# Linear-attention sums for pairs of heads in 32-column blocks, with a second ring of output tiles and a new instruction order

## The chip, the cores and the metric

The kernel runs on one NeuronCore of one Trainium2 chip. The metric is device time in microseconds (us) of one execution, as the median over the executions of one job. A median is over all executions of its job. With one core there are no dies to compare; the mean granted clock of TensorE was 0.981 in the profiled run of the kernel before.

Engines in the profile: PE is TensorE (matrix products), PEld its weight loads, DVE is VectorE, ACT ScalarE, POOL GpSimd, SP SyncE, which here only issues transfers. A name with q is the engine's sequencer or queue.

## The reference, cut to what matters

Four attention layers on x of 2048 x 512, with 32 heads of 16 columns, each behind a layer norm and with a residual. Layers A are softmax attention over a window of 256 positions; layers B are linear attention:

```python
def _B_ref(x, wqkv, wo):
    ...                                        # H = 32 heads, Dh = 16
    phi = lambda t: jnp.where(t > 0, t + 1, jnp.exp(t)) + 1e-6
    pq, pk = phi(q), phi(k)
    kv = jnp.einsum("bhsd,bhse->bhde", pk, v)  # per head a 16 x 16 sum over all positions
    z = jnp.einsum("bhsd->bhd", pk)            # per head the sum of pk
    num = jnp.einsum("bhqd,bhde->bhqe", pq, kv)
    den = jnp.einsum("bhqd,bhd->bhq", pq, z)[..., None] + 1e-6
    ...
x = A_x
x = x + _A_ref(_layernorm(x), A_wqkv, A_wo)
x = x + _B_ref(_layernorm(x), B_wqkv, B_wo)
x = x + _A_ref(_layernorm(x), A_wqkv, A_wo)
x = x + _B_ref(_layernorm(x), B_wqkv, B_wo)
```

The change concerns `kv` and `z` of the two B layers. Only the 16 x 16 blocks of one head are needed, out of the whole 512 x 512 product of pk and v.

## The kernel before

The program is a list of about 2,600 small operations. A planner issues them in the order that a constant text, `ORDER`, lays down (an operation's number, then its engine: P, A, V, G, S). It also keeps a rough clock of its own. Where that clock sees TensorE idle for over 0.45 us, it adds *fillers*: matmuls of the identity whose result nobody reads and which are to keep TensorE's clock up. And it gives each operation one of eight PSUM banks, the one free the earliest by that clock.

```python
        order = ORDER.split()
        for x in order:
            ...
            for s in o.takes:
                start = s.ring.free_at(s, start)[0]      # a PSUM bank or a buffer
            start = max(start, free[e])
            ...
            if e == "PE":
                if start - free["PE"] > self.GAP:        # GAP = .45 us
                    ...
                    fill = (b[0], m) if m else fill
            ...
            self.fill(*fill)
            o.fn(e)
```

The key-value sums of two 128-row tiles form one unit. It computes, for each of four 128-column tiles c, the full 128 x 128 product of pk and v and one column of ones behind it (129 columns), in two halves, each in a PSUM bank of its own and each with its own addition into the float32 sums in SBUF:

```python
        def kv_unit(i):
            ins = [kv_in[i + n] for n in range(2)]
            for jj in range(2):
                s = bank()
                ...
                    for tt in range(2):
                        c = 2 * jj + tt
                        for n in range(2):
                            nc.tensor.matmul(t["t"][:, tt, :], lhsT=ins[n][0][0]["t"][:, c * P:(c + 1) * P],
                                             rhs=ins[n][1][0]["t"][:, c, :], start=(n == 0), stop=(n == 1))
                ...
                    nc.vector.tensor_tensor(kvs[jj][:], t["t"][:], kvs[jj][:], op=ALU.add)
```

Later a block mask (`bd`) keeps the heads' own blocks. The last layer writes its 16 output tiles from one ring of four staging tiles:

```python
            if final:
                ost = slot("xn")
                ...
                pl.op({"SP": .4}, lambda e: nc.sync.dma_start(o_dram[i], t["o"][:]), deps=[r], use=[ost])
```

## Time and profile before

| | before |
|---|---|
| time, median of 3 runs | 477.78 us (477.42 to 478.20) |
| span of the profiled run, granted clock | 477.3 us, 0.981 |
| TensorE busy | 445.7 us, 93% |
| fillers | 48 |
| key-value matmuls, their additions | 128 of 129 columns, 32 of 258 columns |
| TensorE's last matmul ends | 468.8 us |

The prediction below shows the busy shares, the windows and the end. What it names without showing are the large groups and the waits around a shared PSUM bank. In the first fence each line is line of source, engine, operation, output<-input, count, then busy us and mean ns of one, then idle time before them and what ended it.

```profile
L834 ACT ACTIVATE pt<-psb 128x1536 bf16<-128x1536 f32 (+2 forms) x246 | 285.5, 1216 | 32.9 <-PE psb L816 25.1
L816 PE MATMUL psb<-qT,kbd 32*128 32x320 bf16 (+4 forms) x1440 | 94.3, 255 | 4.4 <-ACT pt L834 3.9
L895 PE MATMUL psb<-vbd,pt 128*128 128x34 bf16 x2880 | 84.4, 179 | 0.7 <-POOL pt L867 0.7
```

The 246 exponentials of layers A (L834) take 285.5 us of ScalarE. They come at a steady pace along both A layers, so the start of the 20th, 40th and so on is a good milestone for how far a run has come; I use it below. The B layers' work is laid between them and behind them. The second fence, of the view of waits, has: engine, line, waited for what, us in all, times, longest.

```profile
DVE ost L738 <- DMA out_dram<-ost: 5.8, 5, 2.0
ACT kbd L771 <- DVE kbd L773: 5.1, 2, 3.1
```

The first is the end's wait for a free staging tile. The second is ScalarE waiting for VectorE's half of one bank.

### The profile page before, as it was taken

To read this page: it belongs to the slowest core of one execution; us is meant where nothing else is said; L and a number is where in the kernel's file an instruction comes from. 1 tells how busy PE (TensorE), PEld (TensorE's weight loads), DVE (VectorE), ACT (ScalarE), POOL (GpSimd) and SP (SyncE) were. 2 spreads that over 40 slices of the span, in tenths; PEclk is the share of its full clock that TensorE was granted. 3 is DMA by queue.
4 is the path that set the end of the run, shared out by engine and by line. 5 is a ranking of instruction groups with operands and counts; after the bars stand their busy time and mean duration, and the time that the engine had idled before them with its cause. 6 is when DMAs were issued, how large, how long until landed. Compare 5 with 4: busy or idle time off the path is not lost.

```text
span 477.3 us, 14496 instructions
## 1 busy us (share of the span) xinstructions
PE 445.7 (93%) x5668; PEld 231.3 (48%) x5730; DVE 376.8 (79%) x987; ACT 379.1 (79%) x446; POOL 250.3 (52%) x746
## 2 busy tenths in 40 slices
PE   7789999899999999999999998999999999999991
PEld 2334554464555465543445553545546464655330
DVE  6768787778878977896988786788888887788872
ACT  7488888899998999666578996989988899876610
POOL 4256644547674765351137665477684685561141
PEclk9889999899999999999999998999999999999998
DMA  6313245103240210100010123112411311000023
GB/s 220 111 38 82 58 110 128 35 3 74 50 50 17 43 34 3 46 0 1 6 43 14 26 52 73 29 34 46 71 36 25 57 37 23 2 1 1 0 79 106
DMA packets 53805, 22.27 MB, mean 47 GB/s; under 512 B 38368, under 2 KB 53216, under 8 KB 53728
## 3 DMA queue, kind: packets, MB, share of 16 engines
q1 hardware_dynamic: 49760, 16.80, 16.9%
q10 hardware_dynamic: 3968, 4.46, 3.0%
q8 instruction: 47, 0.77, 0.7%
q14 instruction: 30, 0.25, 0.2%
HBM read 6.29 MB, written 2.10 MB: 18 GB/s over the span
## 4 chain that ended last, share of the span: by engine, by line
PE 71%; DVE 8%; ACT 7%; DMA 6%; POOL 3%; issue 3%; ACTq 0%; SPq 0%; another core or an unknown queue 0%; DVEq 0%; POOLq 0%
PE psb L563 38%; PE psb L895 13%; PE psb L816 13%; ACT pt L834 4%; DMA xnT<-xn 3%; DMA out_dram<-ost 2%; PE psb L1020 2%; POOL pt L867 1%; PE psb L1088 1%; DMA oT<-o_sb 1%; DVE vbd L542 1%; DVE pqT L1119 1%; PE psb L582 1%; PE psb L489 1%; DVE xres L745 1%
## 5 line engine op out<-in xcount | busy, mean ns | idle before, releaser
L834 ACT ACTIVATE pt<-psb 128x1536 bf16<-128x1536 f32 (+2 forms) x246 | 285.5, 1216 | 32.9 <-PE psb L816 25.1
L867 POOL TENSOR_SCALAR_AFFINE_SELECT pt<-pt 128x192 bf16<-128x192 bf16 (+2 forms) x514 | 152.7, 329 | 120.8 <-ACT pt L834 118.6
L816 PE MATMUL psb<-qT,kbd 32*128 32x320 bf16 (+4 forms) x1440 | 94.3, 255 | 4.4 <-ACT pt L834 3.9
L895 PEld LDWEIGHTS <-pt 128*128 128x128 bf16 x2880 | 78.4, 96 | 14.4 <-issue 8.9
L895 PE MATMUL psb<-vbd,pt 128*128 128x34 bf16 x2880 | 84.4, 179 | 0.7 <-POOL pt L867 0.7
L862 DVE TENSOR_TENSOR pt<-pt,tri 128x128 bf16<-128x128 bf16 (+4 forms) x268 | 65.6, 274 | 15.3 <-ACT pt L834 14.0
L816 PEld LDWEIGHTS <-kbd 32*128 32x128 bf16 x1440 | 39.7, 93 | 67.6 <-issue 59.2
L563 PE MATMUL psb<-xnT,wA 128*128 128x512 bf16 x239 | 65.5, 394 | 6.1 <-ACT kbd L771 2.4
L563 PE MATMUL psb<-wB,xnT 128*128 128x512 bf16 x240 | 62.5, 380 | 1.3 <-DVE xnT L585 0.3
L563 PEld LDWEIGHTS <-xnT 128*128 128x128 bf16 x384 | 33.4, 98 | 39.8 <-issue 9.0
L971 ACT ACTIVATE phi_e<-psb 128x512 bf16<-128x512 f32 x64 | 38.1, 603 | 17.1 <-PE psb L563 14.0
L773 DVE TENSOR_TENSOR kbd<-psb,eo 128x512 bf16<-128x512 f32 x57 | 37.1, 681 | 2.7 <-ACT kbd L771 1.9
L563 PEld LDWEIGHTS <-wA 128*128 128x128 bf16 x256 | 21.8, 99 | 34.1 <-issue 15.3
L563 PE MATMUL psb<-wA,xnT 128*128 128x512 bf16 x118 | 33.7, 399 | 1.0 <-DVE xnT L585 0.4
L563 PE MATMUL psb<-woA,oT 128*128 128x512 bf16 x118 | 32.1, 381 | 2.7 <-DMA oT<-o_sb 1.1
L563 PE MATMUL psb<-wkv,pqT 128*128 128x512 bf16 x124 | 30.0, 380 | 2.2 <-DVE ost L738 1.7
L563 PE MATMUL psb<-xnT,wB 128*128 128x512 bf16 x123 | 31.0, 380 | 0.2
L684 DVE BATCH_NORM_STATS2 ln_st<-xres 128x6 f32<-128x512 f32 (+1 forms) x39 | 26.5, 679 | 2.0 <-DMA xres<-in_A_x_dram 1.9
L974 DVE TENSOR_SCALAR phi_e<-phi_e 128x512 bf16<-128x512 bf16 x57 | 18.6, 329 | 9.6 <-ACT phi_e L971 9.2
L910 DVE TENSOR_TENSOR o_sb<-psb,rall 128x384 bf16<-128x384 f32 (+1 forms) x48 | 24.6, 513 | 1.6
L550 DVE CAST qT<-psb 128x512 bf16<-128x512 f32 x27 | 18.5, 686 | 8.0 <-PE psb L563 7.8
L977 DVE SCALAR_TENSOR_TENSOR pqT<-psb,phi_e 128x512 bf16<-128x512 f32 x32 | 21.8, 688 | 1.5 <-POOL phi_e L974 1.0
(121 smaller groups left out, 492.0 us busy)
## 6 DMA issues: line engine op xcount, KB each, us to landing
vbd<-vst SPq DMA_DIRECT2D x128, 34.0 KB, 1.9
out_dram<-ost SPq DMA_DIRECT2D x16, 128.0 KB, 1.8
wB<-in_B_wqkv_dram ACTq DMA_DIRECT2D x1, 1536.0 KB, 7.7
xres<-in_A_x_dram ACTq DMA_DIRECT2D x1, 1024.0 KB, 5.0
xnT<-xn SPq DMA_TRANSPOSE x40, 2.5
wA<-in_A_wqkv_dram SPq DMA_DIRECT2D x1, 512.0 KB, 6.7
xres<-in_A_x_dram SPq DMA_DIRECT2D x1, 512.0 KB, 7.7
woA<-in_A_wo_dram ACTq DMA_DIRECT2D x1, 512.0 KB, 3.5
```

The source lines that it names most:

```text
L563: nc.tensor.matmul(t["t"][:], lhsT=lhs(c), rhs=rhs(c), start=(c == 0), stop=(c == NCT - 1))
L684: nc.vector.bn_stats(t["st"][:], x())
L773: nc.vector.tensor_tensor(kbd[r][:, t, :, :, :].rearrange("p m k h -> p (m k) h"), ps()[:, hf * 256:(hf + 1) * 256].unsqueeze(2).to_broadc ...
L816: nc.tensor.matmul(A[:, x, at[x]:at[x] + w, :], lhsT=kbd[half(m)][32 * rg:32 * rg + 32, tt, m % 4, :, :], rhs=qT[I % 2][32 * rg:32 * rg + ...
L834: nc.scalar.activation(body[:, x:y, 0:pos[x], :], t["A"][:, x:y, 0:pos[x], :], ACT.Exp, scale=0.25)
L862: nc.vector.tensor_tensor(v, v, mt, op=ALU.mult)
L867: nc.gpsimd.affine_select(out=v, in_=v, compare_op=ALU.is_ge, fill=0.0, base=1 if kind == 0 else -2, pattern=[[0, n], [2 * sg, 64]], chann ...
L895: nc.tensor.matmul(t["O"][:, u, g, :, :], lhsT=PT[:, s0:s0 + 2, :], rhs=vbd[half(m)][:, m % 4, :, grp[g], :], start=(n == 0), stop=(n == l ...
L910: nc.vector.tensor_tensor(o_sb[:, u0:u0 + nu, h0 * DH:(h0 + 2 * ng) * DH].rearrange("p u (h e) -> p u h e", e=DH), Ov[:, :, :, 0:DH], r.to ...
L971: nc.scalar.activation(t["e"][:], ps()[:], ACT.Exp)
L974: (nc.vector if e == "DVE" else nc.gpsimd).tensor_scalar(t["e"][:], t["e"][:], 1.0, 1e-6, op0=ALU.min, op1=ALU.add)
L977: nc.vector.scalar_tensor_tensor(out=dst(), in0=ps()[:], scalar=1.0 + 1e-6, in1=t["e"][:], op0=ALU.add, op1=ALU.max)
```

## The change

The intent has three parts. First, the sums are computed only for pairs of heads: for each group of 32 columns a 32 x 32 product and one column of ones (33 columns), in the four column groups of TensorE's array (`tile_position`), so that a unit's result of 132 columns fits in one bank and needs one addition. The column of ones is written once. Second, outputs alternate between two rings of four staging tiles. Third, the whole order is new, and the planner's clock now has it that two engines are not in one bank at once, that an output tile is free only when its transfer has landed (`LAND`), and a few corrected durations.

```diff
-    WIN, FULL, GAP = 3.413, 2750, .45
+    WIN, FULL, GAP, LAND = 3.413, 2750, .45, 1.8
...
+            for s in o.slots:
+                if s.ring is self.banks and s.last and s.last.eng != e:
+                    start = max(start, s.last.end + self.LAT[s.last.eng])
...
 ORDER = """
-19H 17H 18H 20H 36V 37G 46V 6G 47G 12A 51A 41V 42G 23H 38V ...      (all 2,614 operations)
+20H 17H 36V 19H 18H 41V 46V 37G 38V 23H 12A 10V 42G 47G 51A ...      (all 2,582 operations)
...
-        kvs = [fp.tile([P, 2, P + 1], F32, name=f"kvs{j}") for j in range(2)]
+        kvs = fp.tile([P, NCT, 33], F32, name="kvs")
+        vss = [fp.tile([P, NP, 33], BF, name=f"vs{k}") for k in range(3)]
+        for k in range(3):
+            nc.vector.memset(vss[k][:, :, 32:33], 1.0)
...
-                ost = slot("xn")
+                ost = slot(("xn", "oT")[i % 2])
...
-                nc.gpsimd.memset(t["t"][:, :, P:P + 1], 1.0)
...
-            for jj in range(2):
-                s = bank()                                   # [the unit shown above]
+            s = bank()
+                for c in range(NCT):
+                    for g in range(4):
                         for n in range(2):
+                            nc.tensor.matmul(t["t"][32 * g:32 * g + 32, c, :], lhsT=ins[n][0][0]["t"][:, c * P + 32 * g:c * P + 32 * g + 32],
+                                             rhs=ins[n][1][0]["t"][:, 4 * c + g, :], start=(n == 0), stop=(n == 1), tile_position=(0, 32 * g))
...
+                    nc.vector.tensor_tensor(kvs[:], t["t"][:], kvs[:], op=ALU.add)
```

## The prediction

> **What bounds the kernel now.** I read the granted clock first (0.981, one core, so nothing to compare between dies), then the page's busy shares and slices, then the table of windows, the waits, the chain of waits, and last the timeline of the end.
>
> ```profile
> PE 445.7 (93%) x5668; PEld 231.3 (48%) x5730; DVE 376.8 (79%) x987; ACT 379.1 (79%) x446; POOL 250.3 (52%) x746
> ...
> PE   7789999899999999999999998999999999999991
> DVE  6768787778878977896988786788888887788872
> ACT  7488888899998999666578996989988899876610
> ```
>
> TensorE is over 90% busy in nearly every slice except the first three and the last; no other engine is. A busy PE row is modelled, so I checked it against start times in the trace: two 512-column matmuls follow each other every 216 ns, two of the 34-column value products (L895) every 25 ns. Taking such a pace for each form, I counted as a stall whatever exceeds it by more than 0.3 us: 33 stalls, 24.0 us, of which 8.1 us lie before 36 us. So in the middle there is little waiting to win; it is at both ends, and in what TensorE is given to do.
>
> ```profile
> 0.00:60.00 60.00, 50.95 (x540) 23.96 (x547) 44.63 (x112) 45.69 (x61) 29.82 (x110) 0.94 0.37 101
> ...
> 120.00:180.00 60.00, 58.53 (x928) 32.96 (x936) 49.51 (x140) 55.76 (x58) 39.49 (x119) 1.00 0.23 38
> 180.00:240.00 60.00, 58.78 (x494) 28.94 (x501) 49.66 (x124) 40.81 (x75) 20.94 (x51) 1.00 0.04 12
> ...
> 420.00:478.00 58.00, 46.44 (x239) 20.33 (x241) 40.65 (x79) 24.87 (x49) 16.18 (x26) 0.96 0.12 38
> ```
>
> Columns: length, busy us of PE, PEld, DVE, ACT, POOL, clock, DMA. Even where the layers meet (180 to 240) PE is 58.8 of 60, but part of this is filler work (L489, identity matmuls that keep the clock up). The end has 11.6 us without PE.
>
> ```profile
> PE 71%; DVE 8%; ACT 7%; DMA 6%; POOL 3%; issue 3%; ACTq 0%; SPq 0%; another core or an unknown queue 0%; DVEq 0%; POOLq 0%
> ...
> L489 PE MATMUL psb<-identb 128*128 128x512 bf16 x48 | 15.2, 430 | 1.5 <-POOL identb L417 1.5
> ...
> L1020 PE MATMUL psb<-vs,pks 128*128 128x129 bf16 x128 | 11.4, 221 | 0.1
> L1027 DVE TENSOR_TENSOR kvs<-psb,kvs 128x258 f32<-128x258 f32 x28 | 11.5, 421 | 5.4 <-PE psb L1020 5.3
> L1000 POOL MEMSET vs<- x32: 109/114/118, 132.2 to 435.7; 128x4 bf16 x32
> ...
> 466.17 1.29 DVE L738 TENSOR_TENSOR ost<-psb,xres 128x512 bf16<-128x512 f32 x2 [2.00 <-DMA out_dram<-ost]
> 466.92 1.89 PE L563 MATMUL psb<-wkv,pqT 128*128 128x512 bf16 x8 [1.67 <-DVE ost L738]
> 468.72 0.69 DVE L738 TENSOR_TENSOR ost<-psb,xres 128x512 bf16<-128x512 f32 x1 [1.26 <-DMA out_dram<-ost]
> ...
> 469.77 0.69 DVE L738 TENSOR_TENSOR ost<-psb,xres 128x512 bf16<-128x512 f32 x1 [0.36 <-DMA out_dram<-ost]
> 472.05 0.69 DVE L738 TENSOR_TENSOR ost<-psb,xres 128x512 bf16<-128x512 f32 x1 [1.59 <-DMA out_dram<-ost]
> ```
>
> The first line is the page's chain of waits, the next three are groups by line (busy us, mean ns, idle before), the fifth is of the view of the tile vs, the rest is the timeline of the end. The chain is TensorE to 71%. The kvs groups are what the change replaces. The last lines show the end: output tiles wait for an earlier output's transfer to free one of four staging tiles, and at 466.92 even TensorE waits behind that.
>
> **What the Trainium skill says.** (1) "TensorEngine Tiling (Array Packing)", Tiling Modes: changing the tiling mode drains TensorE. The trace agrees: a 512-column matmul is followed after 216 ns by one of its mode, after 311 by one of another, so a change costs 95 ns. From the build's order of TensorE I counted 408 changes in the kernel before, an estimated 39 us. (2) "TensorE: Matmul & The Clock Gate", Back-to-back issue gap: a matmul of 1 to 64 columns costs about a 25 ns floor. The trace's 25 ns for 34 columns agrees, for the full array. Four-column-group work of 32x33 is nowhere in this trace. (3) The tiling page again, Restrictions and Gotchas: column tiling excludes the fast weight load. No run here shows what a 32-column load costs. (4) "PSUM — Partial Sum Buffer", PSUM bank collisions raise a hardware error: two engines must not be in one bank at once, reads included. The trace fits with order being enforced: ScalarE waits 5.1 us in two places for VectorE's half of the same kbd bank (L771 on L773).
>
> **The change, part by part.**
>
> *Key-value sums, TensorE.* Before: 32 units of 4 matmuls, 128 in all, of 129 columns, 57 ns from start to start: 128 x 0.057 = 7.3 us. After, by the build: 512 matmuls of 32x33 in 16 units of 32. At the 25 ns floor: 512 x 0.025 = 12.8 us, so +5.5. This is four times the instructions for a quarter of the columns, so there is no gain on the bound engine. The tile shape is also new, so each unit may drain on entry and exit: the order has 449 mode changes, 32 of them around these units. 41 x 0.095 = +3.9. Sum +9.4 us on the path.
>
> *Key-value sums, the others.* The adds fall from 32 of 258 columns (28 x 421 ns and 4 copies at 416: 13.4 us) to 16 of 132. With 0.96 columns a ns, 258 columns take 269, leaving 152 fixed; so 132 take 290, x 16 = 4.6 us. VectorE loses 8.8 us. GpSimd loses 32 memsets of 114 ns, 3.6 us. Both engines have slack in the windows above; I credit no more than 1 us, as fewer late bank releases. The masking of kvn reads a broadcast instead: same sizes, no change.
>
> *Staging.* Outputs alternate between two rings of four. In the old end, transfers land 1.7 to 3.0 us after issue and about 0.9 us passes between outputs, so eight tiles are plenty. Without these waits TensorE's last matmul would end at 468.8 - 1.8 = 467.0, its addition at 467.7, the transfer about 1.8 later at 469.5, and the closing instructions take the 1.5 us between the last landing (475.8) and the end (477.3): 471.0. That is 6.3 us at most. The remaining VectorE work of this phase may take some back: -5.
>
> *The order.* It is wholly new. Work moves off VectorE (268 masks become 245, the 1.87 us clears of vbd from 3 to 1), to GpSimd (514 to 558 masks) and ScalarE, (two vbd clears become four), which have room in these windows. Fillers fall from 48 to 31; at the meeting of the layers they fall from 18 to 6, at the last one from 6 to 1, because projections now stand between the steps of the closing chain. Real work in their place is worth about 17 x 0.216 = -3.7. The start has 8.1 us of stalls, a part of them from the vbd clears and the kbd halves that the new order is built to know of: -3. The middle: -2.
>
> Sum: +9.4 - 1 - 5 - 3.7 - 3 - 2 = -5.3 us, so 477.8 - 5.3 = 472.5.
>
> **Rivals.** *Column groups run side by side.* For it: the two 64-column groups of the denominators (L1088) run in parallel in this trace:
>
> ```profile
> 442.89 1.06 PE L1088 MATMUL psb<-pqT,zc 128*64 128x512 bf16 x8
> ```
>
> Eight matmuls of 512 columns in 1.06 us is the time of four, with starts 14 ns apart within a pair. If the four groups do the same at 14 ns, the 512 take 7.2 us and the increase of 5.5 vanishes: 467. Against: here two matmuls of one group follow each other before the next group comes. *Weight loads show.* If a load without the fast path isn't hidden, a matmul takes 40 ns: 20.5 us, 8 more: 480. TensorE then becomes the bound even more; the new units stand among attention work and each would delay exponentials. *The end is bound by transfers or by VectorE, not by staging.* The last transfer took 3.0 us, others 1.7; then only 2 to 3 of the 5 come: 475. *The masks on GpSimd arrive late.* It gets about 12 us more of them (44 at about 0.3); L895 waited for them only 0.7 us on PE so far. If the new order is tight there, value products stall by a few us: 475 to 477. I hold this as unlikely, as it has 48% slack.
>
> **Range and chances.** The terms that can be wrong are the pace of the new matmuls (-5.5 to +8), the end (2) and the gain of the order (3). Together some 6 us to either side: 467 to 478.5. Faster by over 2% means below 468.2, which needs parallel column groups, or an order that wins twice what I gave it: 0.15. Slower by over 2% means above 487.3, which needs unhidden loads and no gain elsewhere: 0.02. The rest, 0.83, within 2%.
>
> **What would show it.** The new kvs matmuls: 512, spaced 25 ns, a unit about 0.8 us plus 0.18 of drains (14 ns and 0.45 us for the first rival). The kvs additions near 290 ns. No wait of ost on out_dram, and a last matmul within 5 us of the end. Fillers 31. VectorE's busy time near 360 us, GpSimd's near 258. TensorE's stalls over 0.3 us below 18 us. I'd be wrong if stalls rise in the middle stages, or if the last output still ends 8 us after the last matmul.

## The result, and the profile after

| | before | after |
|---|---|---|
| time, median of 4 runs each | 477.99 us (477.42 to 479.69) | 465.37 us (463.37 to 467.16) |
| ratio, 95% interval | | 0.9729, 0.9681 to 0.9777: faster |
| span of the profiled run | 477.3 | 461.6 |
| TensorE's last matmul ends | 468.8 | 453.8 |

A ratio is the mean time of one kernel's runs over the mean of the other's in the same rounds, so it isn't quite the ratio of the medians. Executions over 1.5% slower than the fastest of the same kernel are left out of the means. A second job with 6 runs of the changed kernel gave 466.91 us and 0.977. The prediction said 472.5 with a range of 467.0 to 478.5: the result lies below the range, in a class that had been given 0.15.

The page of the kernel after, its busy line, its slices, and the chain of waits by engine:

```profile
PE 439.4 (95%) x6097; PEld 226.3 (49%) x6097; DVE 368.0 (80%) x952; ACT 379.9 (82%) x446; POOL 258.0 (56%) x750
...
PE   7998999999999999999999999999999989999893
...
PE 77%; DVE 7%; ACT 7%; DMA 5%; issue 2%; SPq 0%; ACTq 0%; POOL 0%; DVEq 0%
```

VectorE's 368 and GpSimd's 258 us are near what was foretold (360 and 258). TensorE has more instructions than before and is busy for 6 us less (roughly so: the trace of the kernel before lacks 62 matmul records, 5,668 for 5,730 weight loads). The chain of waits went from 71% to 77% TensorE. The windows (length, busy us of PE, PEld, DVE, ACT, POOL, clock, DMA share, GB/s):

```profile
0.00:60.00 60.00, 54.63 (x629) 27.25 (x630) 48.98 (x131) 49.69 (x55) 35.36 (x126) 0.97 0.52 136
...
120.00:180.00 60.00, 59.27 (x1041) 32.61 (x1043) 48.44 (x135) 57.19 (x58) 38.28 (x116) 1.00 0.17 33
180.00:240.00 60.00, 58.98 (x550) 28.97 (x550) 49.97 (x120) 42.46 (x89) 19.43 (x45) 1.00 0.04 10
```

The first minute has 54.6 us of TensorE in place of 51.0, with a clock of 0.97 in place of 0.94. So the start improved before there is any key-value work, which begins at about 134 us. Now the groups that the change replaces:

```profile
L491 PE MATMUL psb<-identb 128*128 128x512 bf16 x31 | 10.3, 455 | 1.5 <-POOL identb L419 1.5
L744 DVE TENSOR_TENSOR ost<-psb,xres 128x512 bf16<-128x512 f32 x11 | 7.3, 688 | 1.8 <-PE psb L569 1.2 <-issue 0.6
L1024 PE MATMUL psb<-vs,pks 128*32 128x33 bf16 x512 | 6.3, 179 | 0.0
L1031 DVE TENSOR_TENSOR kvs<-psb,kvs 128x132 f32<-128x132 f32 x14 | 4.0, 288 | 1.5 <-PE psb L1024 1.5
```

There are 31 fillers. The additions take 288 ns (290 foretold). No output tile waits for out_dram any more. But 512 matmuls are busy for 6.3 us in all, where four times fewer had been busy for 11.4. One unit in the timeline shows why:

```profile
425.78 0.28 PEld L1024 LDWEIGHTS <-pks 128*32 128x32 bf16 x32 [0.42 <-issue]
425.79 0.39 PE L1024 MATMUL psb<-vs,pks 128*32 128x33 bf16 x32
...
426.10 1.41 PEld L569 LDWEIGHTS <-wB 128*128 128x128 bf16 x8
```

All 32 matmuls with their 32 weight loads lie within 0.39 us, of which 0.179 is the length of the last one. In the trace, from the first start of a unit to its last is 0.21 us, 31 intervals of 6 to 7 ns in the mean; where the next matmul waits for nothing, it starts 110 ns after that. The prediction had 0.8 + 0.18 us.

Taking from each start to the next start as the time that a matmul holds TensorE, the key-value units hold it for 7.4 us in all (3.4 within them and 4.0 to what follows, waits there included), against 9.5 before (5.9 and 3.5). What the change of mode costs ahead of a unit falls to the matmul before it. It can be read off a run below, whole_array, which has the same order and no change of mode there: ten of the 16 units then start 93 ns sooner behind the matmul before them, 0.9 us in all. Prediction: +9.4. Measured: -2.0, or an estimated -1.1 with those.

**Where the time went, by stage.** The start times of the 80th, 120th, 140th, 200th and 240th exponential (counted from 0) cut the span into six stretches. Key-value units lie in the second, third, fifth and last stretch; the first and the fourth have none. Each entry is the length in the profiled run, in us.

| profiled run | start to 80 (no kv) | 80 to 120 (kv) | 120 to 140 (kv, layers meet) | 140 to 200 (no kv) | 200 to 240 (kv) | 240 to the end (kv, outputs) | span |
|---|---|---|---|---|---|---|---|
| before | 131.1 | 57.8 | 76.5 | 84.2 | 58.5 | 69.2 | 477.3 |
| after | 124.7 | 56.1 | 77.5 | 80.2 | 57.8 | 65.3 | 461.6 |
| difference | -6.4 | -1.7 | +1.0 | -4.0 | -0.7 | -3.9 | -15.7 |

(The profiled run of the kernel after is the fastest of its four, so the pair differs by 15.7 where the medians differ by 12.6. The first stretch scatters: in six profiled runs whose program is the same up to there (the kernel after twice, and whole_array, group_outer, vector_load and two_queues below) it took 124.7 to 127.7 us.) The gain is in the stretches without key-value work and in the end. The stretches with it are about as long as before, where 8 us of loss were expected.

### The profile page after: what moved, and what is told of

It reads as the page before. It is cut to its first block, busy times and chain, and to the rows that moved or that the text cites.

```text
span 461.6 us, 15250 instructions
## 1 busy us (share of the span) xinstructions
PE 439.4 (95%) x6097; PEld 226.3 (49%) x6097; DVE 368.0 (80%) x952; ACT 379.9 (82%) x446; POOL 258.0 (56%) x750
## 4 chain that ended last, share of the span: by engine, by line
PE 77%; DVE 7%; ACT 7%; DMA 5%; issue 2%; SPq 0%; ACTq 0%; POOL 0%; DVEq 0%
PE psb L569 42%; PE psb L901 15%; PE psb L822 14%; ACT pt L840 5%; DMA oT<-o_sb 3%; DMA wA<-in_A_wqkv_dram 1%; PE psb L588 1%; PE psb L1120 1%; DMA xnT<-xn 1%; DVE xres L751 1%; PE psb L1093 1%; DVE pqT L1124 1%; DVE pqT L983 1%; PE psb L1024 0%; DVE o_sb L916 0%
## 5 line engine op out<-in xcount | busy, mean ns | idle before, releaser
L873 POOL TENSOR_SCALAR_AFFINE_SELECT pt<-pt 128x192 bf16<-128x192 bf16 (+2 forms) x558 | 162.2, 325 | 104.1 <-ACT pt L840 102.9
L868 DVE TENSOR_TENSOR pt<-pt,tri 128x128 bf16<-128x128 bf16 (+4 forms) x245 | 61.9, 283 | 15.3 <-ACT pt L840 15.1
L569 PE MATMUL psb<-xnT,wA 128*128 128x512 bf16 x256 | 63.7, 381 | 1.7 <-DMA xnT<-xn 1.6
L569 PE MATMUL psb<-wB,xnT 128*128 128x512 bf16 x256 | 63.8, 380 | 0.6 <-ACT xnT L591 0.4
L569 PEld LDWEIGHTS <-xnT 128*128 128x128 bf16 x384 | 32.3, 98 | 41.4 <-issue 11.7
L779 DVE TENSOR_TENSOR kbd<-psb,eo 128x512 bf16<-128x512 f32 x60 | 39.1, 683 | 5.4 <-PE psb L569 5.2
L569 PE MATMUL psb<-xnT,wB 128*128 128x512 bf16 x128 | 32.0, 379 | 1.1 <-DVE pqT L983 0.8
L624 POOL TENSOR_TENSOR ln_rs<-ln_rs,mhalf 128x1 f32<-128x1 f32 x39 | 22.8, 584 | 3.2
L915 DVE RECIPROCAL rall<-psb 128x24 f32<-128x24 f32 (+1 forms) x48 | 13.8, 287 | 12.9 <-PE psb L901 12.4
```

The costliest lines, as they stand in the source:

```text
L569: nc.tensor.matmul(t["t"][:], lhsT=lhs(c), rhs=rhs(c), start=(c == 0), stop=(c == NCT - 1))
L624: nc.gpsimd.tensor_tensor(out, out, mhalf[:, 0:1], op=ALU.pow)
L779: nc.vector.tensor_tensor(kbd[r][:, t, :, :, :].rearrange("p m k h -> p (m k) h"), ps()[:, hf * 256:(hf + 1) * 256].unsqueeze(2).to_broadc ...
L868: nc.vector.tensor_tensor(v, v, mt, op=ALU.mult)
L873: nc.gpsimd.affine_select(out=v, in_=v, compare_op=ALU.is_ge, fill=0.0, base=1 if kind == 0 else -2, pattern=[[0, n], [2 * sg, 64]], chann ...
```

## The experiments

Theory 1: the four column groups run side by side, so the prediction's loss on TensorE isn't there, and the rest is about as predicted. Theory 2: it is the new order that wins; it wins twice what it was given, whatever the key-value sums do. Theory 3: VectorE's shorter additions free banks and free VectorE, which the prediction counted as 1 us because VectorE has slack. A further question was whether the parts add.

All kernels gave a correct result except the one named wrong. All time ratios are against the kernel before in the same job, whose median lay between 477.6 and 478.3 in the later jobs.

### The same kernel again, and the same matmuls over the whole array

```diff
 # whole_array: every product over all 128 columns of weights; wrong result on purpose
-    nc.tensor.matmul(t["t"][32 * g:32 * g + 32, c, :], lhsT=...[:, c * P + 32 * g:c * P + 32 * g + 32],
-                     rhs=..., tile_position=(0, 32 * g))
+    nc.tensor.matmul(t["t"][:, c, :], lhsT=...[:, c * P:(c + 1) * P], rhs=...)
```

> The changed kernel unaltered, as the base for the other runs on the same chip. Expected as before: a ratio of 0.973 to the kernel before, 463 to 467 us, TensorE's last matmul about 8 us before the end.

Measured: 466.91 us (464.29 to 468.68), 0.977 [0.974, 0.980]. The gain holds.

> The changed kernel, with the 512 key-value matmuls issued over the whole array (128 weight columns, 33 moving columns, each overwriting the one before it in its columns) instead of on four column groups. The result is wrong on purpose for three of four head pairs; VectorE, ScalarE, GpSimd and the order stay as they are. Theory 1 (the failing term of the prediction is the pace: the four groups run side by side at 6 to 7 ns a matmul, and TensorE is the bound, so its pace counts): the trace shows 25 ns a matmul; 512 x (25 - 6.6) = 9.4 us more, less 32 mode changes of 0.095 = 3.0 us, so about 6.4 us longer than the changed kernel, some 472 us. Rival (the key-value sums lie in gaps of TensorE, their pace hardly counts, the gain is the order's and the other engines'): within 1.5 us of the changed kernel.

Measured: 469.86 us (468.46 to 471.69), 0.982 [0.980, 0.985]. This is the kernel that the prediction had in mind, but for its mode changes, with the same count of matmuls, additions, banks, order and fillers. Its group line:

```profile
L1024 PE MATMUL psb<-vs,pks 128*128 128x33 bf16 x512 | 15.5, 178 | 0.0
```

Starts are 25 ns apart, 0.79 us within a unit, and the units hold TensorE for 14.0 us in place of 7.4. The trace has 19 fewer mode changes (433 for 452); those behind the units are already in the 14.0, those ahead of them save the 0.9 us named above. So 6.5 - 0.9 = 5.6 us more on TensorE cost 2.9 us of time (medians of the same job). The units themselves are 9.2 us longer; some 2 us of that fell into waits that stood behind them anyway. Of the 5.7 us between the profiled runs of whole_array and after_again, 3.4 lie in the three middle stretches with sums and 1.5 in the first, where the programs don't differ. Theory 1 holds for the pace; it explains 3 us, and not all of the miss.

### The pace: who stands beside whom

The same 512 matmuls in another issue order.

```diff
 # group_outer: eight matmuls in a row of one column group
-    for c in range(NCT):
-        for g in range(4):
+    for g in range(4):
+        for c in range(NCT):
             for n in range(2):
```

> The same 512 key-value matmuls, but with the loop over the four column groups outermost, so that eight matmuls in a row are of the same group. If the 6 to 7 ns pace came from neighbours in different groups running side by side, a row of one group runs at 25 ns and a unit of 32 takes about 0.8 us: +6 us on TensorE and +3 us of time, as in the whole-array run. If the groups run ahead of each other whatever the issue order, or if 32 columns are simply faster, the pace stays at 6 to 9 ns and the time stays within 1 us of the kernel after.

Measured: 468.03 us (466.55 to 469.25), 0.981 [0.978, 0.984].

```profile
L1024 PE MATMUL psb<-vs,pks 128*32 128x33 bf16 x512 | 11.7, 179 | 0.0
```

A unit now takes 0.55 us from first to last start in place of 0.21. Within it, starts are 25 ns apart, or 19 and then 6, which I read as a matmul of the next group slipping in early (the trace as kept doesn't name the group). The pace thus depends on the neighbours' groups, and neither extreme of the expectation came: TensorE is held 11.2 us, between 7.4 and 14.0. With the groups innermost (nofill_inner below) four starts come within about 10 ns, then a gap of 15: 25 ns for a round of four. The reading that fits all three orders is that one group takes a 33-column matmul each 25 ns, and four groups do so at once. In time, the run is 2.3 us longer than two_queues of its job, which does not differ from the kernel after (0.975 [0.972, 0.978]).

### The parts taken apart, first attempt: the planner moves

The old sums, or the old staging, in the new kernel. The order is the new one, with the two halves of an old unit where the new unit stood.

```diff
 # oldkv_neworder: kvs, vs, kv_unit and kv_final as before; staging as after
 # oldstaging_neworder
-                ost = slot(("xn", "oT")[i % 2])
+                ost = slot("xn")
```

> The new order and the new staging with the old key-value sums (128 matmuls of 129 columns, 32 additions of 258 columns on VectorE, 32 memsets on GpSimd), correct result; each of the 16 units is put back as two in its place, the order on each engine is else unchanged. Theory 1, by TensorE alone: 7.3 us against 3.4 + 3.0 of mode changes, so about 1 us longer than the changed kernel, and 1 for VectorE: 467 to 468. Rival (the relief of VectorE, 8.8 us, and of GpSimd, 3.6 us, is on the path and was credited with 1 us only): 5 to 9 us longer, 470 to 474.

Measured: 474.38 us (471.44 to 476.33), 0.993 [0.991, 0.996].

> The changed kernel with its outputs staged in one ring of four again, correct result. As the prediction has it: the waits of ost on out_dram return and the end is 5 us later, 470 us. Rival, from the trace of the changed kernel (its last matmul ends at 453.8 of 461.6 us, and one issue of an output's transfer takes 1.76 us on SyncE): the end is now set by SyncE's line of transfers, so staging is worth 1 to 3 us only: 466.5 to 468.5.

Measured: 468.58 us (467.57 to 470.40), 0.980 [0.978, 0.983].

Neither is a clean experiment: the planner saw other durations and put in 61 and 42 fillers in place of 31, and other banks. Who changes one part of such a program changes what is computed from it, too. So I fixed the fillers and the banks in tables.

```diff
 # *_pinned: fillers from a table, banks left to the planner's clock
+                k, m = self.PINNED.get(o.n, (0, 0))
```

> As oldkv_neworder (new order and staging, old key-value sums), but with the fillers of the changed kernel: 31, at the same places, where oldkv_neworder had 61. If the 30 fillers that the first attempt had too many were what cost it (its filler matmuls span 8 us more of TensorE's time than those of the changed kernel), this run comes to 468 to 470 us, 2 to 3 over the changed kernel (3.3 us more of key-value time on TensorE by the trace, and no credit for VectorE). If the relief of VectorE and GpSimd is what counts, it stays at 473 to 475.

> The new order alone: old key-value sums, one staging ring, the 31 fillers of the changed kernel at the same places. By the prediction's terms (3.7 for fillers, 3 for the start, 2 for the middle) 8.7 us under the kernel before, 469. If the parts simply add: oldkv_pinned plus what the old staging costs, so 470 to 473. If the order does nothing by itself and the key-value sums do it all: 476 to 478.

> As oldstaging_neworder (one staging ring), with 31 fillers in place of 42; the 11 more lay in the last phase. If they filled a real wait of TensorE, nothing changes: 468 to 469. If they were in the way, 466 to 467, and the staging is worth nothing in this order.

> The kernel before with the new key-value sums alone, each pair of units made one at the later place, its 48 fillers at the same places, order on each engine else unchanged, correct result. By TensorE's trace alone (10.7 us of old key-value time against 7.4) 1 to 3 us under the kernel before: 475 to 477. If the relief of VectorE is on the path: 470 to 473. If the gain can only be had with the new order: 477 to 479.

Measured: 480.16 us (ratio 1.005), 483.08 (1.012), 474.21 (0.988), and 479.70 (1.004). These runs are not valid for their purpose. The fixed fillers of the start fell into one window of the planner's clock, which then gave other banks to operations at the start, and in the three runs in the new order a scores matmul waited there 3.3 to 3.6 us, as I read it for a bank, which the kernel after doesn't make it wait for. Two of the 22 executions of oldkv_pinned and two of the six of oldstaging_pinned were slow. They did show one thing: the placement of banks alone, with the same order and the same fillers, is worth some 4 us (oldstaging_pinned, its four fast executions 472.9 and 0.988, against 469.19 and 0.979 for oldstaging_placed below).

### The parts taken apart, second attempt: fillers and banks both fixed

The banks are those of the kernel whose order it is, but for some 28 near the key-value units of the old sums, which need one bank more.

```diff
 # *_placed
+                k, m = self.PINNED.get(o.n, (0, 0))
...
+            for n, s in enumerate(o.takes):
+                k = self.PLACES.get(o.n, ())[n:n + 1]     # the bank of the kernel whose order it is
```

> The new key-value sums alone in the kernel before, with its 48 fillers and its PSUM banks. The attempt with other banks gave 479.7, 2 us over the kernel before. If only the banks spoiled it: 474 to 477. If VectorE's and TensorE's relief is of no use in an order that was searched for other lengths: 477 to 480.

Measured (new sums alone, in the old order): 478.92 us (475.98 to 481.77, 14 runs), 1.001 [0.998, 1.004].

> The new order alone: old key-value sums, one staging ring, the fillers and nearly all banks of the changed kernel. If the parts add: oldkv_placed plus 1 to 3 us, so 470 to 476; the order then is worth 2 to 8 us of the 12. If 478 or more, the new order has no gain without the key-value change.

Measured (new order alone, old sums and staging): 484.37 us (482.85 to 486.41), 1.014 [1.010, 1.017].

> Third attempt at the new order and staging with the old key-value sums. The two before were disturbed: one had 61 fillers, the other put many tiles in other PSUM banks than the changed kernel (its planner counted the fillers in the wrong time window), and a scores matmul waited 3 us for a bank at 21 us. Here the 31 fillers and the PSUM banks are those of the changed kernel, but for some 28 banks near the key-value units, which need one bank more. Theory: the key-value change is worth its TensorE time (3.3 us more by the trace, of which half or more counts) and some of VectorE's 8.8 us: 3 to 8 us over the changed kernel, 469 to 474.

Measured (new order and staging, old sums): 479.79 us (477.33 to 483.10, 12 runs), 1.004 [1.002, 1.007], 6 us above the range expected.

> The changed kernel with one staging ring, its 31 fillers and all its PSUM banks as in the changed kernel. The first attempt (42 fillers) was 1.5 to 2 us over the changed kernel. If the staging is worth 5 us as predicted: 471. If the line of transfers on SyncE sets the end in any case: 467.5 to 469.

Measured (all but the staging): 469.19 us (465.72 to 470.31), 0.979 [0.976, 0.983].

The parts do not add. The sums alone win nothing, the order alone loses 1.4%, the order with the staging loses 0.4%, and all together win 2.3 to 2.7%. Theory 2 in its plain form falls: the order isn't better by itself, at least with banks and fillers held. That holding costs something too: oldkv_neworder, where the planner chose banks and fillers for the old sums, took 474.38 us, 5 us less than oldkv_placed. So the old sums cost this order 13 us with all else held and 7.5 us with the planner free (474.38 against 466.91 in one job). The second ring of staging is worth 4.6 us with the old sums (order_placed against oldkv_placed), and with the new ones some 2 us that are not clear of noise (0.979 to 0.980 without it, 0.977 [0.974, 0.980] with it in the second job). The same stretches as above show where:

| profiled run | start to 80 (no kv) | 80 to 120 (kv) | 120 to 140 (kv) | 140 to 200 (no kv) | 200 to 240 (kv) | 240 to the end | span |
|---|---|---|---|---|---|---|---|
| before | 131.1 | 57.8 | 76.5 | 84.2 | 58.5 | 69.2 | 477.3 |
| newkv_placed | 129.6 | 57.6 | 76.3 | 83.8 | 60.2 | 70.1 | 477.6 |
| order_placed | 125.8 | 61.9 | 79.1 | 81.3 | 61.3 | 72.8 | 482.2 |
| oldkv_placed | 127.0 | 61.8 | 79.2 | 80.1 | 62.8 | 67.8 | 478.7 |
| after_again | 126.1 | 56.1 | 77.6 | 80.2 | 57.8 | 64.8 | 462.6 |

Wherever there is no key-value work, all three runs with the new order are 3 to 5 us shorter than the kernel before, with old sums as with new ones. In the three middle stretches that have it, the runs with old sums in the new order are 2.6 to 4.3 us longer than before. The gain of the order is real, and the old sums give it back. How they do so stands in the trace of oldkv_placed. First groups, then a piece of its timeline:

```profile
L569 PE MATMUL psb<-wB,xnT 128*128 128x512 bf16 x235 | 63.3, 387 | 5.9 <-DVE kvs L1031 1.5 <-DVE o_sb L916 1.1 <-DVE kvs L1033 0.7
...
L1026 PE MATMUL psb<-vs,pks 128*128 128x129 bf16 x128 | 11.2, 220 | 4.2 <-DVE kvs L1033 1.9 <-DVE vs L1011 1.3 <-POOL vs L1006 0.4
```

```profile
186.68 0.39 PE L1026 MATMUL psb<-vs,pks 128*128 128x129 bf16 x4
187.53 0.41 DVE L1033 TENSOR_TENSOR kvs<-psb,kvs 128x258 f32<-128x258 f32 x1
187.99 0.39 PE L1026 MATMUL psb<-vs,pks 128*128 128x129 bf16 x4 [0.92 <-DVE kvs L1033]
188.41 0.43 DVE L1033 TENSOR_TENSOR kvs<-psb,kvs 128x258 f32<-128x258 f32 x1 [0.48 <-PE psb L1026]
```

The second half of the unit waits 0.92 us for the first half's addition to be done. Of TensorE's stalls over 0.3 us in this run (32.2 us, against 15.3 in the kernel after), seven of 0.8 to 1.7 us, 7.4 us in all, are ended by such an addition. Others, 5 us in all, are ended by VectorE's copies of v and its normalized outputs (vs, o_sb).

### VectorE's part by itself

The kernel after, with the lost VectorE time put back behind each addition; taking the maximum of the sums with themselves changes no value.

```diff
                     nc.vector.tensor_tensor(kvs[:], t["t"][:], kvs[:], op=ALU.add)
+                for _ in range(2):
+                    nc.vector.tensor_tensor(kvs[:], kvs[:], kvs[:], op=ALU.max)
```

(A first version with a tile of its own didn't build: SBUF had no room left for it.)

> The kernel after with two idempotent maximum operations of kvs with itself behind each of the 16 kvs additions: about 16 x 2 x 0.25 = 8 us more on VectorE at the places where the old, doubled additions stood; nothing changes on TensorE, in the banks or in the order. The theory that the new order works because VectorE's additions became short expects a loss of 4 to 8 us against the kernel after, so 470 to 474, with new TensorE stalls that VectorE ends. The prediction's view (VectorE has slack, 1 us) expects at most 1.5 us, so 466 to 467.5.

Measured: 468.95 us (467.76 to 469.55), 0.983 [0.980, 0.986].

```profile
L1033 DVE TENSOR_TENSOR kvs<-kvs 128x132 f32<-128x132 f32 x32 | 10.1, 316 | 1.1
```

VectorE is busy 376.9 us, 8.9 more than in the kernel after, and the time is 2 to 3 us longer (466.91 for the kernel after in its own job, 465.76 for a kernel of this job that does not differ from it in time, two_queues; by the ratios up to 3.7). TensorE's stalls over 0.3 us go from 16.3 us (after_again) to 20.1. So neither expectation is met: it is more than the 1 us of the prediction and less than Theory 3's 4 to 8. Nor did the stalls come that VectorE ends: none over 0.3 us is ended by an addition or a maximum. What grew are stalls ended by transfers (8.7 us, against 4.3 in after_again), but whole_array has 8.1 of them without this load. On which path VectorE's time becomes time of the kernel is thus not shown. (The maximum does not hold a PSUM bank either, as the longer old addition does.)

So VectorE's time by itself is 2 to 3 of the 13 us that the old sums cost in this order with all else held. (The 2.9 us of whole_array don't belong in this sum: it holds TensorE for 14.0 us, the old sums in their own kernel for 9.5.) Some 5 us go with the held banks and fillers, by oldkv_neworder; the two may overlap. What makes up the rest was not isolated. Candidates are that the old unit takes two banks rather than one, as in the piece of timeline above, GpSimd's 32 memsets, and that the order was made for other durations.

### The fillers

```diff
 # before_nofill, after_nofill: no filler after the first 8 us; banks unchanged
-            self.fill(*fill)
+            if start < 8.0:
+                self.fill(*fill)
```

> The kernel before without the filler matmuls after the first 8 us (order and banks as they were). The prediction counted 216 ns of gained time for each filler that goes, so -3.7 for 17 of them; by that, taking some 36 to 48 away gives -8 us, 470. The rival: fillers stand in waits and cost nothing: 477 to 478.5. If they keep the clock up, taking them away makes more slices with a lower clock and a longer time, over 479.

Measured: 472.55 us (472.16 to 473.96), 0.991 [0.989, 0.994]. The kernel before has 36 fillers that cost it 5 us by the medians, 0.14 us each, and 4 by the ratio (not 0.216 each as the prediction had it, and not nothing, as the rival had it). The granted clock did not fall without them: 0.984 against 0.981.

```profile
L490 PE MATMUL psb<-identb 128*128 128x512 bf16 x12 | 4.6, 560 | 1.5 <-POOL identb L418 1.5
```

> The kernel after without its fillers behind the first 8 us (12 of 31 stay, banks and order unchanged). At the 0.14 us each that the fillers of the kernel before were worth, the 19 that go give -2.7 us: 463 to 464, a ratio near 0.970. If the fillers that are left stand in waits (or keep the clock up), the time stays at 465 to 467.

Measured: 466.15 us (462.42 to 467.79), 0.975 [0.970, 0.980]: no gain. The 19 late fillers that are left in the kernel after cost it nothing that shows; that they stand where TensorE would wait anyway is the likely reading.

> after_nofill with the loop over the column groups innermost in the key-value units, so that no two neighbours are of one group. If side-by-side groups are held up by the second matmul of the same group behind the first, the pace falls from 6 to 7 ns to about 4 and a unit from 0.215 us by some 0.05 us, 16 units: -1 us at most, so within 1 us of after_nofill. If the pace is that of the instruction stream, nothing changes.

```diff
 # nofill_inner: after_nofill, and the groups innermost
-                    for g in range(4):
-                        for n in range(2):
+                    for n in range(2):
+                        for g in range(4):
```

Measured: 465.59 us (463.10 to 467.17), 0.974 [0.969, 0.978], a unit 0.20 us from first to last start in place of 0.21. It isn't faster than the kernel after by more than the runs scatter.

### The end

> The kernel after with 8 of the 16 output transfers issued by ScalarE, the others by SyncE. If the end is held by the line of issues on SyncE (one took 1.76 us), the end after the last matmul shrinks from 7.8 us to about 6 and the time falls by 1 to 2 us, to 464. If the transfers themselves or the additions hold it, the time stays, and issuing on ScalarE may delay its exponentials or copies by up to 0.5 us.

```diff
-  nc.sync.dma_start(o_dram[i], t["o"][:])
+  (nc.scalar if i % 3 == 2 or i % 6 == 3 else nc.sync).dma_start(o_dram[i], t["o"][:])
```

The reason for this run is the end of the kernel after. Its last matmul is 7.8 us before the end of the span, where "within 5" had been foretold:

```profile
452.99 0.69 DVE L744 TENSOR_TENSOR ost<-psb,xres 128x512 bf16<-128x512 f32 x1 [0.17 <-PE psb L569]
453.91 0.69 DVE L744 TENSOR_TENSOR ost<-psb,xres 128x512 bf16<-128x512 f32 x1 [0.23 <-PE psb L569]
455.60 1.26 SPq L746 DMA_DIRECT2D out_dram<-ost  x2
```

```profile
L746 SPq DMA_DIRECT2D out_dram<-ost x16: 332/388/1764, 439.9 to 456.4; - x16
...
DMA to landing us min/median/max: 1.7/1.8/3.8
```

The last addition ends at 454.6, and the last issue starts only at 456.4, since an earlier issue on SyncE took 1.76 us (332 ns is the least); it then lands 3.6 us after that. With two issuing engines:

```profile
L746 ACTq DMA_DIRECT2D out_dram<-ost x8: 337/342/445, 445.3 to 458.1; - x8
L746 SPq DMA_DIRECT2D out_dram<-ost x8: 332/358/447, 448.5 to 457.7; - x8
...
DMA to landing us min/median/max: 1.7/1.8/4.6
```

Measured: 465.76 us (463.09 to 467.20), 0.975 [0.972, 0.978], no gain. No issue takes over 0.45 us now, but the last three transfers take 4.6, 4.1 and 3.9 us to land, and the last matmul is 8.2 us before the end. The line of issues was a symptom: the wait moved from the issue into the transfer. So my theory of the end, that SyncE's issuing holds it, fell. What holds the last transfers for 4 us where the median is 1.8 isn't settled.

No version that I ran beats the kernel after by more than its scatter.

## Why the prediction was right or wrong

**The failed step** is the sum of the key-value part: "At the 25 ns floor: 512 x 0.025 = 12.8 us, so +5.5", with +3.9 of mode changes, "Sum +9.4 us on the path", and 1 us of relief. The pace is 6 to 7 ns, since four column groups run at once, and the units hold TensorE 2.0 us less than before. With the 25 ns put back (whole_array) the kernel takes 469.9, which is inside the range and nearer to the predicted 472.5; so this step alone accounts for 2.9 of the 7.1 us by which the prediction missed. The skill had the mechanism. I took the floor from one section of "TensorE: Matmul & The Clock Gate" (Back-to-back issue gap), while another section of the same page, Part 3: Packing small matmuls, The mechanism, says that tiles run concurrently and gives starts about 4 ns apart (drawn for row groups; here, over column groups, 3 to 5 ns within a round in nofill_inner); and "TensorEngine Tiling (Array Packing)", Key Properties, which I cited for the drain, says in its next point that different tiles can work in parallel. I wrote the case down as the first rival, and set it aside for a reason that isn't one: that two matmuls of one group follow each other. They start 6 to 7 ns apart all the same, since in a row of eight matmuls every group has two, and the groups keep up with each other. The second rival, weight loads that show, did not come; its 40 ns had no trace behind it.

**The mode changes** were counted nearly rightly in the build (449; the trace has 452), and the 110 ns from the last start of a unit to the next matmul fit the 95 ns of a change. But what follows the units came to 4.0 us against 3.5 before, since the old halves had intervals of their own behind them; with the 0.9 us ahead of the units it is +1.4, not +3.9. Five of the 16 units stand behind a matmul of a third mode, so that a change was due there with the old sums too.

**VectorE's relief** was mis-sized at 1 us. VectorE has 20% of idle time, and still 8.9 us put back cost 2 to 3. Idle time in a window's sum doesn't make work free: in oldkv_placed a matmul waits 0.92 us for an addition to be done. (The length of an addition was right, 290 ns against 288. The 0.96 columns a ns behind it came without a source; 421 ns for 258 columns and 288 for 132 give 0.95.)

**The order** came near in size, in part by luck: start -3, middle -2 and fillers -3.7 make -8.7; the stretches without key-value work became 6.4 + 4.0 = 10.4 us shorter in the profiled pair (5.0 + 4.0 with after_again, 5.3 + 2.9 in order_placed). But most of the fillers that went lay in the stretch where the layers meet, which did not become shorter. The unit price of a filler was too high (0.14, not 0.216 us), and the start was worth more than -3, with a scatter of 3 us. ScalarE's wait for VectorE's half of the kbd bank, 5.1 us before, is gone in the three runs of the new order in which I looked for it (after, order_placed, oldkv_placed). What the prediction did not see is that the kernel keeps this gain only with the short sums: with the old ones it lost all of it where banks and fillers were held (479.79), and some two thirds where the planner was free (474.38).

**The end** was in its total close (-3.9 against -5), which is luck in part, since the last stretch holds four key-value units too, and wrong in its reason. The waits for staging tiles went as foretold, but without the second ring the kernel takes 468.6 to 469.2, so staging is worth some 2 us here, not clear of noise; with the old sums it is worth 4.6. The third rival, that transfers bound the end, is nearer to what came; its "others 1.7" was misread, for the trace of the kernel before has landings of up to 3.3 us. "The last output still ends 8 us after the last matmul" was named as what would show me wrong, and it did so (7.8).

**The mean of it:** +8.4 for the sums, -8.7 for order and fillers and -5 for the end made -5.3. Measured in the profiled pair: -1.4 in the three middle stretches with sums, -10.4 in those without, -3.9 in the end. By stretches nearly the whole miss falls to the first term. The experiments isolate less of it: 2.9 us for the pace and some 2 to 3 for VectorE's time, of 7.1. The rest stays open, since the new order works in these stretches too. Stalls over 0.3 us fell from 24.0 to 15.3 us, below the 18 foretold.

## What to carry to other kernels

Before a floor per instruction is multiplied by a count, ask whether neighbours are in different column groups: 33-column products over four groups ran at a quarter of the spacing of the same products over the whole array. In a program with a fixed order, parts of a change don't add: here an order that was made for short operations gained little or nothing without them, so test a part in the order of its own kernel and in that of the other, with banks and fillers held. And idle time in a sum is no proof of slack; put the work back and measure.

## What the Trainium skill lacked or had wrong

- "TensorE: Matmul & The Clock Gate", Back-to-back issue gap, gives a floor of about 25 ns for 1 to 64 columns without saying that it holds per column group. The runs show 25 ns for 33 columns over the whole array or for neighbours of one group, and 6 to 7 ns a matmul over four groups in turn (3 to 5 ns within a round of four, 25 ns from round to round, in nofill_inner).
- The same page, Part 3, The mechanism, says in its list that a weight load overlaps matmuls in flight only when the row group differs, while the paragraph above excepts a load into the background weight buffer. The "only" doesn't fit. Here all loads are of the full 128 rows and differ in column group alone, each matmul has its own load, and 32 of both fit in 0.21 us from first to last start.
- "TensorEngine Tiling (Array Packing)", Key Properties, says that a mode change drains TensorE and gives no duration. The trace shows 95 ns beyond the usual 216 behind a 512-column matmul, and 110 ns from the last 33-column start to the next mode's first.
- No page has that 36 identity matmuls, put in to keep the clock up, cost the kernel before 4 to 5 us, with a granted clock of 0.984 without and 0.981 with them.
